# Ordering the steps of a fused attention and two-layer kernel with a small planner instead of by hand

## The chip, the cores and the metric

The kernel runs on one core of one Trainium2 chip. The time is the device time of one execution in microseconds (us); a kernel's figure is the median of its runs. Four repeats of the kernel before (312.8, 312.04, 312.56 and 313.83 us) count as slow, since they lie over 1.5% above the fastest of their rounds; medians include them, ratios do not. The engines are TensorE (PE in the profile; PEld is its weight load), VectorE (DVE), ScalarE (ACT), GpSimd (POOL) and SyncE (SP, which here issues the loads and the output writes).

## The reference

There are 8 batches of 8 heads, 576 positions and 64 columns. A small set of 32 packed queries `p` first compresses K and V into 32 rows per head; the queries then attend to those 32 rows. The result, 4608 tokens of 512 columns, goes through two layers with a squared ReLU between them.

```python
def sm_attn(qq, kk, vv):
    s = scale * np.matmul(qq, kk.transpose(0, 1, 3, 2))
    a = np.exp(s - np.max(s, axis=-1, keepdims=True))
    a = a / (np.sum(a, axis=-1, keepdims=True) + 1e-09)
    return np.matmul(a, vv)
p_packed = sm_attn(p, k, v)              # 8 x 8 x 32 x 64
x = sm_attn(q, p_packed, p_packed)       # 8 x 8 x 576 x 64, then reshaped to 4608 x 512
r = np.maximum(x @ w_in, 0.0)            # w_in  512 x 2048
out = (r * r) @ w_out                    # w_out 2048 x 512
```

Inputs and outputs are fp32; the kernel multiplies in bf16.

## The kernel before

For every batch the kernel does the same steps, and these names are used below:

- loads of k, v and q; casts to bf16; transposes of k and q on VectorE (`kT`, `qT`);
- scores of `p` against k, then P·V into the PSUM tile `ps_pp`;
- *extraction*: copies from `ps_pp` to `ppT`, the reciprocal sums `rD` and `rD8`, and eight small copies to `pq_bd` (the *pq copies*);
- *M*: the packed rows times `w_in`, so that the first layer works directly on the attention weights. Each of four M steps takes both slots of a two-slot PSUM ring that all attention steps share, and is evicted half by ScalarE and half by VectorE;
- second scores, their normalisation, and then 16 *first-layer* blocks per batch (four matmuls, a ReLU on ScalarE, a square on VectorE into `gT`);
- *second layer*: 36 output tiles of 16 matmuls each, 576 in all.

```python
def extract(self):
    ps = self.ps_pp
    for e in range(2):
        for pr in range(2):
            nc.vector.tensor_copy(self.ppT[64 * e:64 * e + 64, :, pr, :], both(ps, ...)[64 * e:64 * e + 64])
    nc.vector.reciprocal(self.rD, ps[:, 256:258])
    nc.vector.tensor_scalar_mul(self.rD8, self.rD, 0.125)
    for h in range(QH):
        pr, e = divmod(h, 2)
        for dh in range(2):
            s0 = 64 * e + 32 * dh
            dst = bd(self.pq, h, dh)
            if self.b > 1:
                nc.gpsimd.tensor_copy(dst, self.ppT[s0:s0 + 32, :, pr, :])
            else:
                nc.vector.tensor_copy(dst, both(ps, ...)[s0:s0 + 32])

def m(self, c):
    pss = [ps_att.tile([P, 512], F32, name="ps_a", tag="a") for _ in range(NQD)]   # both slots
    for h in range(QH):
        for qd in range(NQD):
            nc.tensor.matmul(pss[qd][o:o + 32, :], lhsT=self.ppT[...], rhs=w_in_b[...], start=True, stop=True)
    ...  # evict pss[0] on ScalarE and pss[1] on VectorE, scaled by rD

def fc1_unit(a, fb):
    ...  # 4 matmuls ps_h <- M, a2
    nc.scalar.activation(r[...], ps[:, :, :HALF], ACT.Relu)
    nc.vector.tensor_tensor(out=g[:, fb, o:o + S], in0=r, in1=r, op=ALU.mult)
```

The order in which steps are issued is written by hand. Lists of steps are spread over fractions of a stage and merged:

```python
def merge(lists):
    tagged = []
    for li, (x, lo, hi) in enumerate(lists):
        for i, f in enumerate(x):
            tagged.append((lo + (hi - lo) * (i + 0.5) / len(x), li, i, f))
    tagged.sort(key=lambda z: z[:3])
    for _, _, _, f in tagged:
        f()
# ... after batch 0's attention and half of its first layer:
merge([(pc[4:], 0.0, 0.02), ([s1[4], s1[7]] + s1[8:], 0.0, 0.25), (fst, 0.06, 0.55),
       ([lambda fb=fb: fc1_unit(a1, fb) for fb in range(NFB)], 0.25, 0.75), (rest, 0.55, 1),
       (pool_casts(L[2])[:2] + [lambda: prep_p(2, B)] + pool_casts(L[2])[2:], 0.55, 0.7),
       (a2.steps(), 0.6, 1.0), (L[3].dma_steps(), 0.6, 0.9)])
for b in range(2, B):          # ... one merge per batch, with fractions of its own
    ...
```

`fst` holds the casts of `w_out` (all on GpSimd), the loads of batch 2 and the second layer's first tiles.

The softmax here doesn't subtract the row's maximum and nothing guards it: scores larger than these inputs give would overflow.

Of the kernel before, what the change touches and what calls it, by code (L numbers as in the profile page):

```python
# [12 lines left out]
P = 128  # L13
D = 64
NP = 32
QH = 4
JT = 18
JP = 3
# [5 lines left out]
class Ctx:  # L24
    pass


def kernel_impl(tc, q, k, v, p, w_in, w_out, out):
# [14 lines left out]
    with ExitStack() as ctx:  # L43
# [125 lines left out]
        class Att:  # L169
            def __init__(self, b, t):  # L170
                self.b, self.t = b, t
                self.kT = att.tile([P, NQD, 2, S], BF16, name="kT", bufs=1)
                self.qT = att.tile([P, NQD, 2, S], BF16, name="qT", bufs=1)
                self.e1 = att.tile([JP * 32, NQD, G, P], BF16, name="e1")
                self.a2 = att.tile([P, NQD, S], BF16, name="a2")
                self.M = mpool.tile([P, NQD, DFF], BF16, name="M")
                self.rD = small.tile([P, NQD], F32, name="rD")
                self.ppT = small.tile([P, NQD, 2, 32], BF16, name="ppT")
                self.rD8 = small.tile([P, NQD], F32, name="rD8")
                self.pq = pq_bd[b % 2]  # L180

            def tr_q(self, qd):
                nc.vector.transpose(  # L183
                    self.qT[:, qd].rearrange("p dh (j a) -> p j dh a", a=32),
                    self.t.q[qd][:].rearrange("p (j dh dl) -> p j dh dl", dh=2, dl=32))

            def tr_k(self, qd):
                nc.vector.transpose(  # L188
                    self.kT[:, qd].rearrange("p dh (g a jp) -> p jp g dh a", jp=JP, a=32),
                    self.t.k[qd][:].rearrange("p (jp g dh dl) -> p jp g dh dl", jp=JP, dh=2, dl=32))  # L190

            def s1(self, qd, hf):
                ps = ps_att.tile([P, 512], F32, name="ps_a", tag="a")
                for gi in range(3):
                    g = hf * 3 + gi
                    for dh in range(2):
# [3 lines left out]
                                         start=(dh == 0), stop=(dh == 1))  # L200
                nc.scalar.activation(self.e1[:, qd, 3 * hf:3 * hf + 3, :], ps[:JP * 32, :3 * P],
# [18 lines left out]
            def extract(self):  # L220
                ps = self.ps_pp
# [7 lines left out]
                for h in range(QH):  # L229
                    pr, e = divmod(h, 2)  # L230
                    for dh in range(2):
                        s0 = 64 * e + 32 * dh
                        dst = bd(self.pq, h, dh)
                        if self.b > 1:
                            nc.gpsimd.tensor_copy(dst, self.ppT[s0:s0 + 32, :, pr, :])  # L235
                        else:
                            nc.vector.tensor_copy(  # L237
                                dst, both(ps, pr * 64 + 32 * e, P + (-32 if e else 32), 32)[s0:s0 + 32])

            def m(self, c):  # L240
                pss = [ps_att.tile([P, 512], F32, name="ps_a", tag="a") for _ in range(NQD)]
# [26 lines left out]
            def norm(self, qd, hf):  # L268
# [4 lines left out]
                nc.scalar.activation(ls, ps[:, :HALF], ACT.Ln)  # L273
                rs = small.tile([P, HALF], F32, name="rs", bufs=2)
                nc.scalar.activation(rs, ls, ACT.Exp, scale=-1.0)  # L275
                nc.vector.tensor_tensor(out=self.a2[:, qd, hf * HALF:(hf + 1) * HALF], in0=e2, in1=rs, op=ALU.mult)

            def kparts(self):
                return ([lambda: (expand_p(self.b, nc.vector if self.b == 0 else nc.gpsimd), self.tr_k(0)),
                         lambda: self.tr_k(1)]  # L280
                        + [lambda qd=qd, hf=hf: self.s1(qd, hf) for qd in range(NQD) for hf in range(2)])

            def steps(self):
                kp = self.kparts()
                ms = [lambda c=c: self.m(c) for c in range(NWC)]
                s2s = [lambda qd=qd, hf=hf: self.s2(qd, hf) for qd in range(NQD) for hf in range(2)]
                ns = [lambda qd=qd, hf=hf: self.norm(qd, hf) for qd in range(NQD) for hf in range(2)]
                st = [kp[0], kp[1], kp[2], kp[3], lambda: self.tr_q(0), kp[4], kp[5], lambda: self.tr_q(1)]
                st += [lambda: self.pv(0),
                       lambda: (self.pv(1), self.extract()), nop, nop, nop, ms[0], s2s[0], s2s[1], ms[1], ns[0],  # L290
                       s2s[2], ns[1], ms[2], s2s[3], ns[2], ms[3], ns[3], nop]
                return st
# [17 lines left out]
        def fc2_steps(t, alt=False):  # L310
            g = gT
# [3 lines left out]
            def mm(fb):  # L315
                if fb == 0:
                    st.ps = (ps_att.tile([P, NE], F32, name="ps_oa", tag="a") if alt
                             else ps_o.tile([P, NE], F32, name="ps_o", tag="o"))
                nc.tensor.matmul(st.ps, lhsT=g[:, fb, n0:n0 + P], rhs=w_out_b[:, fb, :],  # L319
# [9 lines left out]
            return [lambda fb=fb: mm(fb) for fb in range(NFB)]  # L329

        def merge(lists):
            tagged = []
            for li, (x, lo, hi) in enumerate(lists):
                for i, f in enumerate(x):
                    tagged.append((lo + (hi - lo) * (i + 0.5) / len(x), li, i, f))
            tagged.sort(key=lambda z: z[:3])
            for _, _, _, f in tagged:
                f()

        def nop():  # L340
            return None

        V, A, Q = nc.vector, nc.scalar, nc.gpsimd

        def pool_casts(ld):
            return ([lambda qd=qd: ld.cast_kq("k", qd, (Q,)) for qd in range(NQD)]
                    + [lambda qd=qd: ld.cast_v(qd, (Q,)) for qd in range(NQD)]
                    + [lambda qd=qd: ld.cast_kq("q", qd, (Q,)) for qd in range(NQD)])

        L = [Loads(b) for b in range(B)]  # L350
        load_p(0, 2)
        setup()
        prep_p(0, 2)
        for f in L[0].dma_steps():
            f()
        for c in range(QH):
            dma_w_in(0, c)
        a0 = Att(0, L[0])
        kp = a0.kparts()
        L[0].cast_kq("k", 0, (A, Q))  # L360
        kp[0]()
        L[0].cast_kq("k", 1, (A, Q))
        kp[2]()
        kp[1]()
        kp[3]()
        L[0].cast_v(0, (Q, V))
        kp[4]()
        L[0].cast_v(1, (Q, V))
        kp[5]()
        a0.pv(0)  # L370
        a0.pv(1)
        L[0].cast_kq("q", 0, (A, Q))
        a0.tr_q(0)
        a0.extract()
        L[0].cast_kq("q", 1, (A, Q))
        a0.tr_q(1)
        cast_w_in(0, 0, Q)
        cast_w_in(0, 1, V)
        cast_w_in(0, 2, Q)
        a0.s2(0, 0)  # L380
        a0.s2(0, 1)
        a0.s2(1, 0)
        cast_w_in(0, 3, V)
        a0.norm(0, 0)
        a0.norm(0, 1)
        a0.s2(1, 1)
        a0.norm(1, 0)
        a0.norm(1, 1)
        for c in range(QH):
            dma_w_in(1, c)  # L390
        for f in L[1].dma_steps():
            f()
        a0.m(0)
        a0.m(1)
        c1 = [lambda c=c: cast_w_in(1, c, Q) for c in range(3)]
        merge([([lambda fb=fb: fc1_unit(a0, fb) for fb in range(8)], 0, 1), (c1, 0, 1)])
        cast_w_in(1, 3, V)
        a0.m(2)
        a0.m(3)
        for c in range(4):  # L400
            dma_w_out(c)
        a1 = Att(1, L[1])
        s1 = a1.steps()
        pc = pool_casts(L[1])
        merge([([lambda fb=fb: fc1_unit(a0, fb) for fb in range(8, 16)], 0, 1),
               (pc[:2], -0.1, 0.4), (s1[:4] + s1[5:7], 0.2, 1), (pc[2:4], 0.5, 0.8)])
        fs = [fc2_steps(t, alt=False) for t in range(4)]
        fst = []
        for c in range(NFB // 2):
            def chunk(c=c):  # L410
                cast_w_out(c, Q)
                if c + 4 < NFB // 2:
                    dma_w_out(c + 4)
                if c == 3:
                    for f in L[2].dma_steps():
                        f()
                    load_p(2, B)
            fst.append(chunk)
            for t in range(2):
                for fb in (2 * c, 2 * c + 1):  # L420
                    fst.append(fs[t][fb])
        a2 = Att(2, L[2])
        rest = [nop, nop] + fs[2] + [nop, nop] + fs[3]
        merge([(pc[4:], 0.0, 0.02), ([s1[4], s1[7]] + s1[8:], 0.0, 0.25), (fst, 0.06, 0.55),
               ([lambda fb=fb: fc1_unit(a1, fb) for fb in range(NFB)], 0.25, 0.75), (rest, 0.55, 1),
               (pool_casts(L[2])[:2] + [lambda: prep_p(2, B)] + pool_casts(L[2])[2:], 0.55, 0.7), (a2.steps(), 0.6, 1.0), (L[3].dma_steps(), 0.6, 0.9)])
        cur, done = a2, 4
        for b in range(2, B):
            lists = [([lambda fb=fb: fc1_unit(cur, fb) for fb in range(NFB)], 0, 1)]
            avail = (b * S) // P  # L430
            if b + 1 < B:
                nxt = Att(b + 1, L[b + 1])
                if b == 2:
# [62 lines left out]
```

## Time and profile before

| | before |
|---|---|
| time, median | 310.55 us (3 runs, 309.9 to 312.8) |
| profiled span | 306.3 us |
| second-layer matmuls started by 110 us | 80 of 576 |

The first view is the profile page. Part 1 gives busy time, share of the span and instruction count; in part 2 each digit is one fortieth of the span (7.66 us here) in tenths of busy time, or of full clock.

```profile
PE 255.9 (84%) x1920; PEld 141.5 (46%) x1920; DVE 184.0 (60%) x306; ACT 179.7 (59%) x329; POOL 104.0 (34%) x178
...
PE   0647466689687989989999999999999999999993
...
PEclk9999969579999999999999999999999999999998
DMA  7979998950378259974188216751111121121232
```

TensorE stands at 8 or 9 tenths from the fourteenth slice on. Before that it does not, and the DMA row stays at 7 to 9 for eight slices, drops to 0 at about 69 to 77 us and comes back. The next view splits this kernel into three windows: window, length, then busy time of each engine, mean granted clock, DMA share and GB/s.

```profile
core 0: us, PE busy (x) PEld busy (x) DVE busy (x) ACT busy (x) POOL busy (x), PEclk, DMA share, GB/s
0.00:60.00 60.00, 31.14 (x245) 17.41 (x246) 41.54 (x78) 26.70 (x48) 33.68 (x47) 0.90 0.93 299
60.00:110.00 50.00, 40.04 (x296) 20.96 (x296) 29.09 (x46) 30.37 (x57) 19.00 (x35) 0.95 0.49 138
110.00:280.00 170.00, 163.17 (x1279) 93.02 (x1277) 111.41 (x179) 116.70 (x216) 51.35 (x96) 1.00 0.42 120
```

Here is TensorE's timeline of the kernel before around 100 us (start, duration, engine, line, operation, count, and in brackets the idle time before it and what ended it):

```profile
98.03 0.71 PE L246 MATMUL ps_a<-w_in_b,ppT 64*32 64x512 bf16 x8 [0.35 <-ACT e_1137 L264]
98.67 0.39 PE L319 MATMUL ps_o<-w_out_b,gT 128*128 128x512 bf16 x1
99.53 0.40 PE L260 MATMUL ps_a<-qT,pq_bd_101 128*128 128x288 bf16 x2 [0.47 <-ACT M L252]
```

From the start of M (L246) to the next start is 0.64 us. Then one second-layer matmul runs, and TensorE stands idle for 0.47 us.

A last reading, of waits on GpSimd in the kernel before (engine and line, what it waited for, us in total, times, longest), with GpSimd's timeline in the same kernel below it:

```profile
POOL pT_bd_99 L78 <- DVE pT L102: 14.2, 1, 14.2
```

```profile
81.51 1.78 POOL L78 COPY pT_bd_99<-pT 32x64 bf16<-32x64 bf16 x8 [14.19 <-DVE pT L102]
83.35 3.01 POOL L78 CAST v_b<-v_f 96x1536 bf16<-96x1536 f32 x2
```

GpSimd stands from about 67 to 81.5 us for a transpose of `p` that VectorE does late, and batch 2's v casts and batch 3's loads (first issued at 82.9 us) come after it.

### The profile page before, as it was taken

The numbers are of one execution on the slowest core, as the hardware profiler recorded it, in microseconds if no ns is written. First come the engines' busy times: TensorE is split into PE (matmuls) and PEld (weight loads), VectorE is DVE, ScalarE is ACT, GpSimd is POOL, SyncE is SP. The second block draws the span as 40 slices with busy tenths as digits, with TensorE's granted clock in tenths as the row PEclk, the third lists the DMA queues.
The fourth block names the chain that finished last, engine by engine and source line by source line (L and its number), as shares of the span: only waits on it lengthen the run. The fifth ranks groups of instructions, "written<-read, shape, count | busy, mean of one in ns | idle before, by whom it ended". The sixth has DMA issues, their size and how long they took to land.

```text
span 306.3 us, 5208 instructions
## 1 busy us (share of the span) xinstructions
PE 255.9 (84%) x1920; PEld 141.5 (46%) x1920; DVE 184.0 (60%) x306; ACT 179.7 (59%) x329; POOL 104.0 (34%) x178
## 2 busy tenths in 40 slices
PE   0647466689687989989999999999999999999993
PEld 0513234135352455445655555456545654555441
DVE  3785869534784485749685959587867634432100
ACT  3435455276566655786578647865786578655220
POOL 4443885410369404910492039202940200000000
PEclk9999969579999999999999999999999999999998
DMA  7979998950378259974188216751111121121232
GB/s 251 344 264 342 311 320 298 252 176 0 79 228 245 60 146 277 334 194 144 46 248 264 64 39 189 197 198 35 37 34 36 45 60 35 34 61 44 61 78 69
DMA packets 23353, 47.00 MB, mean 153 GB/s; under 512 B 5408, under 2 KB 11552, under 8 KB 23328
## 3 DMA queue, kind: packets, MB, share of 16 engines
q1 hardware_dynamic: 22800, 46.54, 51.4%
q8 instruction: 15, 0.25, 0.4%
q10 hardware_dynamic: 528, 0.13, 0.2%
q14 instruction: 10, 0.08, 0.1%
HBM read 37.22 MB, written 9.44 MB: 152 GB/s over the span
## 4 chain that ended last, share of the span: by engine, by line
PE 49%; DVE 18%; ACT 13%; DMA 8%; issue 4%; SPq 3%; POOL 3%; ACTq 0%; POOLq 0%; DVEq 0%
PE ps_o L319 24%; PE ps_h L302 14%; DVE kT L188 6%; DVE gT L308 5%; ACT r L306 4%; DMA kq_f<-in_q_dram 3%; PE ps_a L246 3%; PE ps_a L198 3%; ACT M L252 3%; SPq L328 3%; PE ps_a L260 2%; ACT o_sb L323 2%; DMA out_dram<-o_sb 2%; DVE qT L183 2%; DMA kq_f<-in_k_dram 2%
## 5 line engine op out<-in xcount | busy, mean ns | idle before, releaser
L319 PE MATMUL ps_o<-w_out_b,gT 128*128 128x512 bf16 x576 | 159.2, 382 | 0.0
L308 DVE TENSOR_TENSOR gT<-r 128x576 bf16<-128x576 bf16 x128 | 74.5, 586 | 65.9 <-ACT r L306 64.8
L306 ACT ACTIVATE r<-ps_h 128x576 bf16<-128x576 f32 x128 | 82.9, 651 | 44.4 <-PE ps_h L302 41.6
L319 PEld LDWEIGHTS <-gT 128*128 128x128 bf16 x576 | 54.3, 98 | 46.0 <-issue 11.5
L302 PEld LDWEIGHTS <-M 128*128 128x128 bf16 x512 | 50.8, 100 | 32.6 <-issue 2.4
L252 ACT ACTIVATE M<-ps_a,rD 128x512 bf16<-128x512 f32 x32 | 22.0, 687 | 20.9 <-PE ps_a L246 20.3
L188 DVE STREAM_TRANSPOSE kT<-k_b 128x1152 bf16<-128x1152 bf16 x16 | 32.9, 2077 | 0.0
L323 ACT COPY o_sb<-ps_o 128x512 f32<-128x512 f32 x36 | 20.8, 581 | 18.4 <-PE ps_o L319 9.7
L246 PE MATMUL ps_a<-w_in_b,ppT 64*32 64x512 bf16 x256 | 20.9, 428 | 12.5 <-DVE ppT L224 3.7
L254 DVE TENSOR_SCALAR M<-ps_a,rD 128x512 bf16<-128x512 f32 x32 | 23.8, 744 | 9.1 <-PE ps_a L246 9.1
L198 PEld LDWEIGHTS <-kT 128*96 128x96 bf16 x192 | 15.1, 132 | 24.8 <-DVE kT L188 21.8
L78 POOL CAST v_b<-v_f 96x1536 bf16<-96x1536 f32 (+1 forms) x16 | 23.4, 1478 | 5.0 <-DMA v_f<-in_v_dram 4.9
L235 POOL COPY pq_bd_102<-ppT 32x64 bf16<-32x64 bf16 x24 | 6.0, 250 | 51.8 <-DVE ppT L224 50.8
L183 DVE STREAM_TRANSPOSE qT<-q_b 128x1152 bf16<-128x1152 bf16 x16 | 21.9, 1371 | 2.5 <-POOL q_b L78 2.5
L78 POOL CAST k_b<-kq_f 128x1152 bf16<-128x1152 f32 (+1 forms) x16 | 18.3, 1162 | 6.7 <-DMA kq_f<-in_k_dram 6.4
L198 PE MATMUL ps_a<-pT_bd_99,kT 128*96 128x128 bf16 x96 | 9.1, 244 | 13.6 <-DVE kT L188 13.6
L235 POOL COPY pq_bd_101<-ppT 32x64 bf16<-32x64 bf16 x24 | 5.9, 245 | 41.4 <-DVE ppT L224 40.4
L78 POOL CAST q_b<-kq_f 128x1152 bf16<-128x1152 f32 (+1 forms) x16 | 19.1, 1210 | 1.2 <-DMA kq_f<-in_q_dram 1.2
L246 PEld LDWEIGHTS <-ppT 64*32 64x32 bf16 x256 | 5.4, 90 | 30.1 <-issue 20.4
L273 ACT ACTIVATE ls<-ps_a 128x288 f32<-128x288 f32 x32 | 13.1, 409 | 3.7 <-PE ps_a L271 3.1
L275 ACT ACTIVATE rs<-ls 128x288 f32<-128x288 f32 x32 | 14.2, 443 | 1.0
L260 PE MATMUL ps_a<-qT,pq_bd_101 128*128 128x288 bf16 x32 | 7.5, 322 | 7.1 <-DVE pq_bd_101 L237 4.1
(178 smaller groups left out, 253.6 us busy)
## 6 DMA issues: line engine op xcount, KB each, us to landing
kq_f<-in_k_dram SPq DMA_DIRECT2D x16, 576.0 KB, 5.3
v_f<-in_v_dram SPq DMA_DIRECT2D x16, 576.0 KB, 6.9
kq_f<-in_q_dram SPq DMA_DIRECT2D x16, 576.0 KB, 8.1
out_dram<-o_sb SPq DMA_DIRECT2D x144, 64.0 KB, 1.7
w_f<-in_moe_w_in_dram SPq DMA_DIRECT2D x8, 512.0 KB, 9.5
w_f<-in_moe_w_out_dram SPq DMA_DIRECT2D x8, 512.0 KB, 7.2
p_f<-in_p_dram SPq DMA_DIRECT2D x1, 384.0 KB, 14.4
p_f<-in_p_dram ACTq DMA_DIRECT2D x1, 128.0 KB, 4.1
```

Source lines behind the costliest of these rows:

```text
L78: eng.tensor_copy(dst, src)
L183: nc.vector.transpose(self.qT[:, qd].rearrange("p dh (j a) -> p j dh a", a=32), self.t.q[qd][:].rearrange("p (j dh dl) -> p j dh dl", dh=2 ...
L188: nc.vector.transpose(self.kT[:, qd].rearrange("p dh (g a jp) -> p jp g dh a", jp=JP, a=32), self.t.k[qd][:].rearrange("p (jp g dh dl) -> ...
L198: nc.tensor.matmul(ps[:JP * 32, gi * P:(gi + 1) * P], lhsT=lhsT, rhs=pT_bd[self.b % 2][:, (qd * 2 + dh) * P:(qd * 2 + dh + 1) * P], start= ...
L246: nc.tensor.matmul(pss[qd][o:o + 32, :], lhsT=self.ppT[64 * e:64 * e + 64, qd, pr, :], rhs=w_in_b[64 * e:64 * e + 64, qd * 2 + pr, c * WCH ...
L252: nc.scalar.activation(dst, pss[e], ACT.Copy, scale=self.rD[:, e:e + 1])
L254: nc.vector.tensor_scalar_mul(dst, pss[e], self.rD[:, e:e + 1])
L302: nc.tensor.matmul(ps[:, c, :HALF], lhsT=a.M[:, qd, fb * FB:(fb + 1) * FB], rhs=a.a2[:, qd, c * HALF:(c + 1) * HALF], start=(qd == 0), sto ...
L306: nc.scalar.activation(r[:].rearrange("p (c n) -> p c n", c=2), ps[:, :, :HALF], ACT.Relu)
L308: nc.vector.tensor_tensor(out=g[:, fb, o:o + S], in0=r, in1=r, op=ALU.mult)
L319: nc.tensor.matmul(st.ps, lhsT=g[:, fb, n0:n0 + P], rhs=w_out_b[:, fb, :], start=(fb == 0), stop=(fb == NFB - 1))
L323: nc.scalar.copy(o_sb, st.ps)
```

## The change

The hand order goes. Each step becomes a `Step` with durations per engine, dependencies by name, and buffer slots that it takes and gives. While the program is built, `Plan` keeps a clock for each engine queue and each slot, looks at the head of every stream, and issues the step that can start earliest on its *first* engine, or the one of best priority within 0.03 us of that. Nothing of it runs on the chip.

```diff
+class Plan:
+    def start(self, st):
+        e = st.segs[0][0]
+        t = self.free.get(e, 0.0)
+        for d in st.deps:
+            if d not in self.done:
+                return INF
+            t = max(t, self.done[d] + HOP)
+        for p, n in st.take:
...
+    def commit(self, st, t):
...
+        for seg in st.segs:
+            side = seg if isinstance(seg, list) else [seg]
+            for e, us in side:
+                b = max(t, self.free.get(e, 0.0))
+                self.free[e] = b + us          # later segments book later engines at once
...
+        st.fn()
+    def run(self):
...
+            at = [(self.start(x[1][0]), x[0], i) for i, x in enumerate(live)]
+            t0 = min(a[0] for a in at)
+            t, _, i = min((a for a in at if a[0] <= t0 + self.near), key=lambda a: (a[1], a[0]))
+            self.commit(live[i][1].pop(0), t)
...
-                        if self.b > 1:
-                            nc.gpsimd.tensor_copy(dst, self.ppT[s0:s0 + 32, :, pr, :])
-                        else:
-                            nc.vector.tensor_copy(
-                                dst, both(ps, pr * 64 + 32 * e, P + (-32 if e else 32), 32)[s0:s0 + 32])
+                        nc.vector.tensor_copy(
+                            dst, both(ps, pr * 64 + 32 * e, P + (-32 if e else 32), 32)[s0:s0 + 32])
...
+            return [Step(f"F1.{b}.{fb}", [("PE", 0.49), ("ACT", 0.66), ("DVE", 0.48)], lambda fb=fb: fc1_unit(T[b], fb),
+                         [f"M.{b}.{fb // 4}"] + [f"N.{b}.{qd}.{hf}" for qd in range(NQD) for hf in range(2)]
+                         + ([f"F2.{t}.{fb}" for t in ...] if b > 1 else []),
+                         [("h", 1), ("r", 1)], [("h", 1, 1), ("r", 2, 1)]) for fb in range(NFB)]
...
+        ld = load_steps(0) + w_in_load(0) + w_in_load(1) + load_steps(1) + w_out_load()
...
+        plan.stream(2, w_in_cast(0, (Q, V, Q, V)) + w_in_cast(1, (Q, V, Q, V)) + w_out_cast((Q, V)))
+        plan.stream(3, [x_step(b) for b in range(B)])
+        plan.stream(3, sum([tr_steps(b, "k") + tr_steps(b, "q") for b in range(B)], []))
+        plan.stream(4, sum([s1_steps(b) + pv_steps(b) for b in range(B)], []))
+        plan.stream(5, sum([m_steps(b) for b in range(B)], []))
+        plan.stream(5, sum([s2_steps(b) for b in range(B)], []))
+        plan.stream(6, sum([f1_steps(b) for b in range(B)], []))
+        plan.stream(7, sum([fc2_steps(t) for t in range(NT)], []))
+        est = plan.run()
```

Three placements change with it. Of the 16 weight casts VectorE (V) now does 8 instead of 3, and GpSimd (Q) 8 instead of 13. The pq copies of batches 2 to 7 go from GpSimd to VectorE, where they read PSUM. And GpSimd's halves of batch 0's k, q and v casts go to VectorE (k, q) and ScalarE (v).

## The prediction

> **What bounds the kernel now.** TensorE's own work, plus an early stretch in which it starves. Unit costs from the timeline: second layer 32 matmuls in 6.92 us = 0.216 us each; first layer 0.49 us per block of four; M projection 0.64 us per eight; scores 0.37 us per six; P·V 1.0 us per batch; second scores 0.24 us; norm 0.12 us. (The Trainium skill, "TensorE: Matmul & The Clock Gate", "Wait — 56ns, not 53.3ns?": N/2.4 + 2.5 ns, 215.8 ns at N = 512; the trace agrees.) Sum, an estimate: 576×0.216 + 128×0.49 + 32×(0.64+0.37+0.24+0.12) + 8×1.0 ≈ 239 us.
>
> By 110 us (windows view) only 87 of 576 second-layer matmuls, 145 of 512 first-layer ones and three batches of attention are done, about 55 us of work: some 54 us are lost. After it, 184 us of work takes 192 us; a batch period (K transpose to K transpose) is 30-32 us against 29.9 us of work: at most 8 us to gain.
>
> The early loss has a hard part: loads run at 299 GB/s over 0-60 us, DMA engines 93% busy, and the last w_out cast ends at 54.4 us; the order of loads stays, so second-layer work can't start in earnest before 48-54 us. And a soft part: batch 1's attention runs at 45-68 us, its first layer mostly at 68-90 us at a granted clock of 0.72-0.79 over 40-70 us. POOL then idles 67-81 us because pT's transpose stands late in VectorE's order; behind it batch 2's casts, batch 3's loads (83 us) and batch 2's first layer (103.7 us) are late.
>
> **What the change does.** Same arithmetic and buffers; the order is a greedy list schedule, each step as early as inputs and slots allow, second-layer matmuls as filler. Half of the weight casts from POOL to VectorE (about 1.1 us each); batches 2-7's eight pq copies from POOL (0.25 us each) to VectorE (0.22 us). VectorE then carries about 24 us per batch (estimate: kT 4.1, qT 2.7, gT 9.4, M 3.0, ppT and pq 2.8, norm 2.4), ScalarE 23 us, both under 29.9 us: off the critical path.
>
> **On the critical path.** With w_out in at 52 us, TensorE can by then have done batch 0 (14 us), batch 1's attention, part of its first layer and one second-layer tile: about 28 us. The other 211 us, and the 8 us loss end near 271 us; tail 5 us; the plain time lies 4 us above the profiled span (310.55 against 306.3), 1 us of slip: 281 us. So 30 of the 54 us come back.
>
> **Prediction: 281 us, 269 to 298.** Faster by over 2%: 0.91; within 2%: 0.06; slower: 0.03.
>
> **Right if:** second-layer matmuls done by 110 us rise from 87 to about 170; granted clock near 1.0 by 55-60 us; batch 2's first layer starts at 65-80 us; batch 3's loads issue before 75 us; POOL's 14 us wait on the pT transpose is gone; batch period still 30-32 us; DMA share over 0-50 us still 0.9. **Wrong if** the gain sits in the batch period.
>
> **What would make it wrong.** The plan's durations are short of the trace's: M 0.40 against 0.64 us, K transpose 1.4 against 2.05, gT 0.48 against 0.59, loads faster than 299 GB/s, output writes free. VectorE is strict FIFO (same page, first table), so a w_out cast placed too early there blocks squares and transposes behind it; output writes queue behind loads.

## More of the kernel before

The busy figures of TensorE must not be read as work. The ends of matmuls are modelled, so overlapping ones count waiting and filling as busy.

## The result, and the profile after

| | before | after |
|---|---|---|
| time, median (same rounds) | 310.23 us (4 runs) | 291.3 us (4 runs) |
| ratio, 95% interval | | 0.9413 (0.9314 to 0.9511) |
| profiled span | 306.3 us | 289.3 us |
| second-layer matmuls by 110 us | 80 | 129 |
| GpSimd's wait for the transpose of `p` | 14.2 us | 1.6 us |

A ratio is the mean time of one kernel's fast runs over the mean of the other's of the same rounds, so it isn't quite the ratio of the medians. Here it leaves out the 312.8 us of the kernel before.

The same rows of the page, of the changed kernel (a slice is 7.23 us):

```profile
PE 251.1 (87%) x1920; PEld 139.7 (48%) x1920; DVE 192.2 (66%) x363; ACT 177.2 (61%) x331; POOL 78.6 (27%) x119
...
PE   0526884789999999999998999999998999999993
...
PEclk9999997879999999999999999999999999999999
DMA  7977999999969693155049960271120201120222
```

The DMA row no longer has a hole before 110 us, and TensorE's row reaches 9 in the tenth slice. The early slices are hardly better. The windows of the changed kernel say the same:

```profile
0.00:60.00 60.00, 32.58 (x253) 18.40 (x254) 46.42 (x86) 27.21 (x48) 22.41 (x35) 0.94 0.92 292
60.00:110.00 50.00, 48.76 (x418) 26.40 (x415) 39.21 (x74) 34.64 (x69) 28.31 (x48) 0.97 0.91 267
110.00:280.00 170.00, 165.18 (x1239) 93.07 (x1240) 106.57 (x205) 114.22 (x213) 27.85 (x36) 1.00 0.32 91
```

And TensorE's timeline of the changed kernel, in a stretch of M steps:

```profile
64.14 0.41 PE L314 MATMUL ps_a<-w_in_b,ppT 64*32 64x512 bf16 x8
64.48 2.12 PE L370 MATMUL ps_o<-w_out_b,gT 128*128 128x512 bf16 x9
66.53 0.41 PE L314 MATMUL ps_a<-w_in_b,ppT 64*32 64x512 bf16 x8
66.87 1.90 PE L370 MATMUL ps_o<-w_out_b,gT 128*128 128x512 bf16 x8
```

Here an M step takes 0.34 us from its start to the next start, not 0.64 (of all 32 M steps 22 do so, in the kernel before 12), and eight or nine second-layer matmuls fill the 2 us until the next M can have its two slots. No idle time is shown.

**Where the time came from.** To compare runs, I count the work that TensorE has done by a given time, as an estimate worked out from the traces: each matmul that has started counts the time from its start to the next start where nothing waits. That is 0.2155 us for a second-layer matmul, 0.49 for a first-layer block, 0.342 for an M step, 0.335 for six score matmuls, 0.243 and 0.122 for a second score and a norm, and 1.0 for a batch's P·V. The sum is 576×0.2155 + 128×0.49 + 32×(0.342 + 0.335 + 0.243 + 0.122) + 8×1.0 = 228.2 us. What a stretch has beyond the work done in it is lost time:

| us lost by TensorE, profiled run | 0 to 60 us | 60 to 110 us | 110 us to the last matmul |
|---|---|---|---|
| before | 42.9 | 16.7 | 13.8 |
| after | 40.6 | 5.1 | 10.6 |

The change takes 17.1 us out: 2.3 before 60 us, 11.6 between 60 and 110, and 3.2 after. A part of this loss is the clock. A stretch's length times the missing share of its mean granted clock (0.90 and 0.95 before, 0.94 and 0.97 after) is 6.2 and 2.3 us before, 3.4 and 1.7 us after, and nothing from 110 to 280 us in either; as an estimate, that is the most that the clock took. So the 2.3 us gained before 60 us may be the clock alone.

The first 60 us are nearly as bad as they were, and the steady part still loses 10.6 us. The experiments ask about these two remainders, and about what was gained. In some traces of the experiments up to 33 of the 1920 matmul records are missing; their counts are scaled up by kind, so differences under about 1 us in this measure mean nothing.

### The profile page after: what moved, and what is told of

Same layout as the page of the kernel before. It is cut to its first block, busy times and chain, and to the rows that moved or that the text cites. A ratio compares the mean times of both kernels' runs of the same rounds, so it can differ in the third digit from the quotient of the medians.

```text
span 289.3 us, 5225 instructions
## 1 busy us (share of the span) xinstructions
PE 251.1 (87%) x1920; PEld 139.7 (48%) x1920; DVE 192.2 (66%) x363; ACT 177.2 (61%) x331; POOL 78.6 (27%) x119
## 4 chain that ended last, share of the span: by engine, by line
PE 61%; DVE 24%; ACT 7%; DMA 3%; issue 2%; SPq 1%; DVEq 0%
PE ps_o L370 30%; PE ps_h L355 19%; DVE kT L254 7%; PE ps_a L314 4%; DVE gT L361 3%; ACT r L359 3%; PE ps_a L264 2%; DVE pq_bd_101 L304 2%; PE ps_a L328 2%; DVE qT L248 2%; DVE pq_bd_102 L304 2%; DVE ppT L294 2%; DMA out_dram<-o_sb 2%; DMA p_f<-in_p_dram 1%; PE ps_pp L279 1%
## 5 line engine op out<-in xcount | busy, mean ns | idle before, releaser
L370 PE MATMUL ps_o<-w_out_b,gT 128*128 128x512 bf16 x576 | 153.0, 385 | 5.8 <-DVE w_out_b L145 2.4
L361 DVE TENSOR_TENSOR gT<-r 128x576 bf16<-128x576 bf16 x128 | 67.0, 536 | 34.3 <-ACT r L359 32.3
L359 ACT ACTIVATE r<-ps_h 128x576 bf16<-128x576 f32 x128 | 79.8, 653 | 14.7 <-PE ps_h L355 9.7
L355 PEld LDWEIGHTS <-M 128*128 128x128 bf16 x512 | 48.7, 98 | 27.0 <-issue 7.0
L374 ACT COPY o_sb<-ps_o 128x512 f32<-128x512 f32 x36 | 20.9, 582 | 30.7 <-PE ps_o L370 19.3
L145 POOL CAST k_b<-kq_f 128x1152 bf16<-128x1152 f32 x14 | 16.1, 1152 | 56.4 <-DVE kT L254 45.1
L145 POOL CAST q_b<-kq_f 128x1152 bf16<-128x1152 f32 x14 | 15.9, 1144 | 43.9 <-issue 42.1
L145 POOL CAST v_b<-v_f 96x1536 bf16<-96x1536 f32 x14 | 20.4, 1469 | 7.3 <-DMA v_f<-in_v_dram 6.3
L314 PE MATMUL ps_a<-w_in_b,ppT 64*32 64x512 bf16 x256 | 17.3, 412 | 5.3 <-DVE pq_bd_102 L304 1.8
L248 DVE STREAM_TRANSPOSE qT<-q_b 128x1152 bf16<-128x1152 bf16 x16 | 21.2, 1349 | 0.0
L344 ACT ACTIVATE rs<-ls 128x288 f32<-128x288 f32 x32 | 14.2, 443 | 1.0
L294 DVE CAST ppT<-ps_pp 64x64 bf16<-64x64 f32 x32 | 5.7, 217 | 11.6 <-PE ps_pp L284 11.5
L355 PE MATMUL ps_h<-a_285,M 128*128 128x288 bf16 x64 | 10.6, 305 | 0.9 <-ACT r L359 0.6
## 6 DMA issues: line engine op xcount, KB each, us to landing
p_f<-in_p_dram SPq DMA_DIRECT2D x1, 384.0 KB, 13.8
```

The lines of the kernel that those rows point to most:

```text
L145: eng.tensor_copy(dst, src)
L248: nc.vector.transpose(self.qT[:, qd].rearrange("p dh (j a) -> p j dh a", a=32), self.t.q[qd][:].rearrange("p (j dh dl) -> p j dh dl", dh=2 ...
L314: nc.tensor.matmul(pss[qd][o:o + 32, :], lhsT=self.ppT[64 * e:64 * e + 64, qd, pr, :], rhs=w_in_b[64 * e:64 * e + 64, qd * 2 + pr, c * WCH ...
L355: nc.tensor.matmul(ps[:, c, :HALF], lhsT=a.M[:, qd, fb * FB:(fb + 1) * FB], rhs=a.a2[:, qd, c * HALF:(c + 1) * HALF], start=(qd == 0), sto ...
L359: nc.scalar.activation(r[:].rearrange("p (c n) -> p c n", c=2), ps[:, :, :HALF], ACT.Relu)
L370: nc.tensor.matmul(st.ps, lhsT=gT[:, fb, n0:n0 + P], rhs=w_out_b[:, fb, :], start=(fb == 0), stop=(fb == NFB - 1))
```

## The experiments

All kernels but the last computed the right result. The starting point for most is the changed kernel, which was run once more, unedited, beside the second group. e1, e2, e5 and e8 shared one chip; a_control, e3, e4 and e10 another; e13, e15 and e16 a third; e17 a fourth. Across chips the ratios are compared, not the times.

| run | edit | median us | ratio to before, 95% | lost 0–60 | 60–110 | after 110 |
|---|---|---|---|---|---|---|
| a_control | none | 292.46 | 0.9455 (0.9383 to 0.9528) | 40.7 | 7.0 | 10.5 |
| e3_pq_pool | pq copies back on GpSimd | 284.28 | 0.9184 (0.9106 to 0.9262) | 41.6 | 5.4 | 4.0 |
| e16_pq_sbuf | pq copies on VectorE, from SBUF | 293.64 | 0.9481 (0.9439 to 0.9523) | 41.1 | 5.6 | 12.6 |
| e15_before_pq_dve | before, pq copies on VectorE | 313.79 | 1.0142 (1.0099 to 1.0185) | 43.4 | 22.6 | 14.6 |
| e5_before_p_early | before, `p` prepared early | 309.33 | 1.0013 (0.9929 to 1.0098) | 42.8 | 19.5 | 15.0 |
| e1_kt_early | batch 1's k transposes earlier | 294.69 | 0.9564 (0.9486 to 0.9642) | 41.2 | 13.9 | 7.2 |
| e2_wo_pool | `w_out` casts on GpSimd only | 293.25 | 0.9514 (0.9460 to 0.9568) | 41.9 | 4.8 | 11.8 |
| e8_kt_wo | both of these | 288.99 | 0.9351 (0.9282 to 0.9421) | 38.3 | 4.6 | 8.7 |
| e4_vq_act | batch 1's v, q casts on ScalarE | 291.07 | 0.9415 (0.9339 to 0.9491) | 40.1 | 5.6 | 10.0 |
| e10_ld_wo | e2 and batch 1's k, v loaded earlier | 293.27 | 0.9506 (0.9409 to 0.9602) | 40.1 | 5.0 | 13.3 |
| e13_kt_wo_pq | e8 and e3 | 282.00 | 0.9115 (0.9069 to 0.9160) | 38.8 | 4.1 | 4.3 |
| e17_no_wout | e1 and e3, no `w_out` (wrong) | 284.99 | 0.9230 (0.9200 to 0.9259) | 37.8 | 5.9 | 7.6 |

The record's verdict at 2% is "faster" for e1, e2, e8, e13, e16 and e17, "same" for e5 and e15, and "unclear" for the four runs on the chip of a_control, where two of the seven repeats of the kernel before were slow. Those four are therefore compared with each other.

### Question 1: what does the move of the pq copies to VectorE cost?

The prediction held that VectorE, with 24 us of work in a batch of about 30, had room for them. The opposite reading, which is not the rival written down for e3: they stand in the middle of a chain from P·V to the next transposes and evictions, in an engine that works in order, and cost time there.

**e3_pq_pool**, the copies back on GpSimd; the plan's durations and so its order are untouched.

```diff
-                        nc.vector.tensor_copy(
-                            dst, both(ps, pr * 64 + 32 * e, P + (-32 if e else 32), 32)[s0:s0 + 32])
+                        if self.b > 1:
+                            nc.gpsimd.tensor_copy(dst, self.ppT[s0:s0 + 32, :, pr, :])
+                        else:
+                            nc.vector.tensor_copy(
+                                dst, both(ps, pr * 64 + 32 * e, P + (-32 if e else 32), 32)[s0:s0 + 32])
```

> Undo one part: the eight pq copies of batches 2-7 go back to POOL, nothing else moves. As predicted (off the critical path): within 1.5 us of the control. Rival: these copies sit between P.V and the second scores of every batch, POOL does them behind its casts, and the time rises by 2-5 us.

Measured: 284.28 us against the control's 292.46 on the same chip, 8.2 us less; the two intervals of the ratios lie apart. Both branches of the expectation missed: one had the time within 1.5 us, the other 2 to 5 us longer. Of the 7.2 us between the two profiled runs 6.5 are after 110 us, where the lost time falls from 10.5 to 4.0 us. One extraction shows how. First VectorE in the changed kernel (start, duration, engine, line, operation, count), then TensorE in it:

```profile
148.69 0.73 DVE L294 CAST ppT<-ps_pp 64x64 bf16<-64x64 f32 x4
...
150.28 1.85 DVE L304 CAST pq_bd_101<-ps_pp 32x64 bf16<-32x64 f32 x8
152.16 2.10 DVE L254 STREAM_TRANSPOSE kT<-k_b 128x1152 bf16<-128x1152 bf16 x1
154.29 0.75 DVE L322 TENSOR_SCALAR M<-ps_a,rD 128x512 bf16<-128x512 f32 x1
```

```profile
151.20 0.39 PE L314 MATMUL ps_a<-w_in_b,ppT 64*32 64x512 bf16 x1
152.18 0.41 PE L314 MATMUL ps_a<-w_in_b,ppT 64*32 64x512 bf16 x7 [0.60 <-DVE pq_bd_101 L304]
```

The same place with the copies on GpSimd (e3_pq_pool), VectorE and then TensorE:

```profile
149.31 0.73 DVE L294 CAST ppT<-ps_pp 64x64 bf16<-64x64 f32 x4
...
150.35 2.10 DVE L254 STREAM_TRANSPOSE kT<-k_b 128x1152 bf16<-128x1152 bf16 x1
152.32 0.75 DVE L325 TENSOR_SCALAR M<-ps_a,rD 128x512 bf16<-128x512 f32 x1
```

```profile
151.81 0.41 PE L317 MATMUL ps_a<-w_in_b,ppT 64*32 64x512 bf16 x8
```

In the changed kernel VectorE is in the extraction from 148.69 to 152.16, 3.5 us, where the plan counts 2.0. M needs both PSUM slots and `ps_pp` still holds one, so all but its first matmul wait until the last pq copy has read it. The transpose of k, which is next in VectorE's order, and M's eviction behind that start late too. From the first `ppT` copy to M's eviction is 5.60 us (154.29 − 148.69); with the copies on GpSimd it is 3.01 us (152.32 − 149.31). This isn't the same in every batch: over batches 2 to 7 the difference is 2.6, −0.4, 2.6, 0.7, 2.6 and 0.7 us, 8.8 us in all. That is near the 8.2 us gained, but that each of these us delays TensorE isn't shown.

**e16_pq_sbuf** parts two explanations: the held PSUM slot, or VectorE's time. The copies stay on VectorE but read `ppT` in SBUF, so that the slot is free once `ppT` and `rD` are read.

```diff
-                        nc.vector.tensor_copy(
-                            dst, both(ps, pr * 64 + 32 * e, P + (-32 if e else 32), 32)[s0:s0 + 32])
+                        nc.vector.tensor_copy(dst, self.ppT[s0:s0 + 32, :, pr, :])
```

> Edit to the changed kernel: the eight pq copies stay on VectorE, but read the SBUF copy ppT instead of PSUM. Putting them back on POOL gained 8 us (ratio 0.918 against 0.9455 of the control). Slot theory: the loss comes from holding the P.V accumulator, one of two attention PSUM slots, for 1.85 us longer, so that the M projection's second half waits (about 0.99 us in the trace); reading ppT frees it, and most of the 8 us come back: ratio 0.918-0.93, 285-288 us. Load theory: it's the 1.85 us of VectorE time itself ahead of the transposes and M's evictions: ratio 0.938-0.947, 291-293 us. In between if the SBUF copies are shorter than 0.22 us each.

Measured: 293.64 us, ratio 0.9481, no gain over the control (0.9455); the load theory is the nearer one, though its range ended at 0.947. VectorE and TensorE in e16_pq_sbuf:

```profile
150.82 3.23 DVE L304 COPY pq_bd<-ppT 32x64 bf16<-32x64 bf16 x8
154.09 2.07 DVE L254 STREAM_TRANSPOSE kT<-k_b 128x1152 bf16<-128x1152 bf16 x1
```

```profile
151.74 0.41 PE L313 MATMUL ps_a<-w_in_b,ppT 64*32 64x512 bf16 x8
156.22 1.40 PE L264 MATMUL ps_a<-pT_bd,kT 128*96 128x128 bf16 x12 [2.23 <-DVE kT L254]
```

M no longer waits: its eight matmuls run as one group. But the transpose still comes late, and now the scores wait 2.23 us for it. So the slot by itself isn't what the 8 us hang on; VectorE's order is the explanation left. The experiment isn't clean, since in this place the eight copies took 3.23 us instead of 1.85, beside casts on GpSimd. Its profiled run also had a granted clock of 0.98 from 110 to 280 us, which by the estimate above is up to 3.4 of the 12.6 us lost there. What it shows is that freeing the slot doesn't bring the time back while VectorE is occupied as long or longer.

**e15_before_pq_dve** does this part of the change alone, on the kernel before: the branch for GpSimd is removed, as in the diff of the change.

> One part of the change alone, on the kernel before: its eight pq copies of batches 2-7 go from POOL to VectorE, order as it was. If the copies are costly in themselves: slower by 3-8 us, 313-318 us. If they are costly only in the planned order, where the M projection is placed to start as soon as the plan thinks P.V done: within 2 us of 310 us, since the hand order has three empty steps between P.V and M.

Measured: 313.79 us against 309.91, 1.4% slower; the six runs lie above all eleven of the kernel before. The profiled run can't place the cost. It loses its extra time between 60 and 110 us (22.6 against 16.7), but its granted clock was 0.83 there against 0.95, which by the estimate above is up to 8.6 us against 2.3. The clock isn't the whole difference: at 0.954 over the whole run e15 took 314.0 us, the kernel before 311.07. From the first `ppT` copy to M's eviction e15 takes longer in batch 2 alone (4.26 us against 1.48), and up to 0.3 us less or the same in the five batches after it. In the hand order, then, the copies lengthen this chain once and not in the steady part.

### Question 2: did GpSimd's 14 us wait cause the late batches?

The prediction reads the wait as the cause of the late casts, loads and first layer of batch 2. The rival: everything there is late for other reasons, and GpSimd merely stands in line.

**e5_before_p_early**, on the kernel before: `p` of batches 2 to 7 is loaded and prepared early.

```diff
             dma_w_in(1, c)
+        load_p(2, B)
         for f in L[1].dma_steps():
...
         cast_w_in(1, 3, V)
+        prep_p(2, B)
         a0.m(2)
...
-                    load_p(2, B)
...
-               (pool_casts(L[2])[:2] + [lambda: prep_p(2, B)] + pool_casts(L[2])[2:], 0.55, 0.7), ...
+               (pool_casts(L[2]), 0.55, 0.7), ...
```

> Edit to the kernel before: p of batches 2-7 is loaded ahead of batch 1's data and its cast and transpose stand in the queues before batch 0's third M projection, nothing else. If the 60-110 us stretch of the kernel before was lost to the late pT transpose (POOL idle 67-81 us behind it), batch 2's attention moves up by 5-10 us and the time falls to 301-306 us. Rival (the hand order loses there for other reasons: batch 3's loads behind output writes, M projections of batch 1 and 2 running one by one): less than 3 us gained, 308-311 us.

Measured: 309.33 us, the same as before (308.03 on that chip). The profiled run was the slowest of the four (312.3 us), with a granted clock of 0.87 from 60 to 110 us against 0.95; but at like clocks over the whole run (0.964 and 0.965) e5 took 307.71 us and the kernel before 307.82. GpSimd's timeline of e5_before_p_early answers to the two lines shown for the kernel before:

```profile
63.34 2.32 POOL L78 COPY pT_bd<-pT 32x64 bf16<-32x64 bf16 x8
65.72 1.46 POOL L78 CAST v_b<-v_f 96x1536 bf16<-96x1536 f32 x1
```

The wait is gone and the v casts stand at 65.7 us instead of 83.35. Still the k transpose of batch 2 came at 84.5 us (before: 81.3) and the loads of batch 3 at 86.5 (before: 82.9). The wait was the longest single one on GpSimd, and its removal gained nothing. That the hand order itself places those steps (`a2.steps()` and `L[3].dma_steps()` stand at 0.6 of the merge and later) is read from the code, not tested.

### Question 3: what holds the first 60 us?

Both kernels lose over 40 us there. In the changed kernel, batch 1's k is cast by 36.1 us, but its transposes run at 47.6 and 50.1 us, behind squares of batch 0. VectorE of the changed kernel, and before it GpSimd of the same kernel:

```profile
32.22 1.15 POOL L145 CAST k_b<-kq_f 128x1152 bf16<-128x1152 f32 x1 [1.77 <-DMA kq_f<-in_k_dram]
34.98 1.15 POOL L145 CAST k_b<-kq_f 128x1152 bf16<-128x1152 f32 x1 [1.62 <-DMA kq_f<-in_k_dram]
```

```profile
37.02 10.02 DVE L361 TENSOR_TENSOR gT<-r 128x576 bf16<-128x576 bf16 x12
46.97 0.68 DVE L145 CAST w_out_b<-w_f 128x1024 bf16<-128x1024 f32 x1
47.57 2.08 DVE L254 STREAM_TRANSPOSE kT<-k_b 128x1152 bf16<-128x1152 bf16 x1
```

Theory S, starvation in the plan: a first-layer step begins on TensorE and is ranked by its start there, although its square books VectorE at once, so such steps are taken before a transpose that begins on the busy VectorE. The plan's own figures show this for batch 1: it has k ready at 28.0 us and its transpose at 40.3. (The plan's own end is 266.6 us, 22.7 under the profiled span.) Theory P: twelve squares take 10.02 us, 0.84 each, because GpSimd's casts block them, and that is the delay. Theory F, from the prediction: a floor, since the second layer can't start in earnest before `w_out` is loaded and cast.

**e1_kt_early** tests S: the last eight first-layer blocks of batch 0 wait for batch 1's k transposes.

```diff
-                         [f"M.{b}.{fb // 4}"] + ...
+                         ([f"Tk.1.{fb // 4 - 2}"] if b == 0 and fb >= 8 else []) + [f"M.{b}.{fb // 4}"] + ...
```

> Edit: in the changed kernel's plan, blocks 8-11 of batch 0's first layer must come after batch 1's first K transpose, blocks 12-15 after its second. Theory S (starvation: a step that begins on TensorE always looks earlier than one that begins on VectorE, so batch 1's transposes stand behind all sixteen squares of batch 0): the first K transpose of batch 1 starts at 34-38 us instead of 47.6, batch 1's first layer at 62-68 us instead of 74.7, and the time falls by 4 to 8 us, to 283-287 us. Rival D (data: w_out and batch 1's loads come late, so the order in the first 60 us doesn't matter): the transposes move, the time stays within 2 us of 291. The plan itself now puts the last w_out cast later, which works against the gain.

Measured: 294.69 us, not better than the changed kernel. The transposes did come earlier (42.4 and 44.3 us), and batch 1's first layer at 66.3 us instead of 74.7. But the last `w_out` cast on VectorE ended at 68.9 us (59.4 in the changed kernel), only 9 second-layer matmuls were done by 60 us instead of 17, and the stretch from 60 to 110 us lost 13.9 us instead of 5 to 7.

**e2_wo_pool** takes the `w_out` casts off VectorE.

```diff
-... + w_out_cast((Q, V)))
+... + w_out_cast((Q,)))
```

> Edit: all eight w_out casts on POOL instead of POOL and VectorE in turn. Theory S: the last w_out cast ends at 55-57 us instead of 59.4, batch 1's K transposes start perhaps 1 us earlier, and the time changes by less than 3 us, since the transposes still stand behind the squares. Rival D: w_out is what TensorE waits for in the first 60 us, so its earlier casts show in full, 2-4 us. Rival P (POOL's casts hold back VectorE's squares): more POOL casts, slower by 1-3 us.

Measured: 293.25 us, no gain. The last `w_out` cast ended at 54.9 us, batch 1's k transpose still only at 49.6 us.

**e8_kt_wo** is both edits together.

> Both edits together (K transposes of batch 1 early, w_out casts on POOL). Theory S: the gain of the first edit without its drawback: batch 1's first layer starts at 60-66 us, 22 us of work done by 60 us rise to 27-30, time 280-285 us. Rival D: within 3 us of 291 us, or the gain of the w_out edit alone.

Measured: 288.99 us, ratio 0.9351 against 0.9413 and 0.9455 of the two runs of the changed kernel. The intervals overlap, so this is a hint, and the time also lies within rival D's 3 us. VectorE in e8_kt_wo shows the transposes in place:

```profile
36.83 4.08 DVE L361 TENSOR_TENSOR gT<-r 128x576 bf16<-128x576 bf16 x4
40.84 3.99 DVE L254 STREAM_TRANSPOSE kT<-k_b 128x1152 bf16<-128x1152 bf16 x2
```

Though they are 6.7 us earlier, TensorE's work by 60 us is up by only 2.3 us (21.7 against 19.4). Theory S is true of the plan, and a small part of the loss.

**e4_vq_act** tests P: the v and q casts of batch 1 go from GpSimd to ScalarE, after batch 0's first layer.

```diff
+        who = lambda b: (A, V) if b == 0 else (A,) if b == 1 else (Q,)
+        cs = {b: cast_steps(b, "k", ...) + cast_steps(b, "v", who(b)) + cast_steps(b, "q", who(b)) for b in range(B)}
+        for st in cs[1][2:]:
+            st.deps.append(f"F1.0.{NFB - 1}")
```

> Edit to the changed kernel: batch 1's v and q casts run on ScalarE after batch 0's last first-layer block instead of on POOL; VectorE's order in the first 60 us stays the same but for one swap. Theory P (in the first 60 us VectorE is late because POOL's casts hold back its squares: in the changed kernel the 22 squares that overlap a POOL instruction take 0.91 us, the others 0.457): the sixteen squares of batch 0 end at 40-42 us instead of 47, batch 1's first K transpose starts at 41-43 us instead of 47.6, and the time falls by 2-5 us. Theory S alone (the order of the queue is what matters): the transpose starts no earlier than 45 us, time within 1.5 us of the control.

Measured: 291.07 us against the control's 292.46, no difference. Here is VectorE in e4_vq_act:

```profile
41.67 1.00 DVE L361 TENSOR_TENSOR gT<-r 128x576 bf16<-128x576 bf16 x2 [0.39 <-ACT r L359]
...
46.20 2.09 DVE L254 STREAM_TRANSPOSE kT<-k_b 128x1152 bf16<-128x1152 bf16 x1
```

The squares that no GpSimd instruction overlaps take about 0.46 us each, and now they wait for ScalarE's ReLUs, which take 0.65 to 0.70 us a block. The transpose came at 46.2 us instead of 47.5 in the control. The blocking is real but not the limit, because ScalarE is right behind it.

That it is real shows in the changed kernel's trace: of its 128 squares the 22 that overlap a GpSimd instruction by more than 50 ns take 0.913 us on average, the other 106 take 0.457. In the kernel before it is 0.867 (41 squares) and 0.454 (87). The Trainium skill, "SBUF — State Buffer", section "SBUF: two separate sides", says that the port pair shared by VectorE and GpSimd is "an exclusive lock, not a bandwidth split", and counts a VectorE operation with two SBUF inputs among those that take it against a GpSimd operation that reads SBUF. A square has two SBUF inputs and a cast reads SBUF, so the trace agrees.

**e10_ld_wo** brings batch 1's k and v in before the second half of `w_in`.

```diff
-        ld = load_steps(0) + w_in_load(0) + w_in_load(1) + load_steps(1) + w_out_load()
+        l1 = load_steps(1)
+        ld = load_steps(0) + w_in_load(0) + l1[:4] + w_in_load(1) + l1[4:] + w_out_load()
```

(with e2's edit)

> Edit to the changed kernel: batch 1's k and v are loaded before the second half of w_in, and w_out casts all run on POOL. This gives batch 1's K transposes a free VectorE by arrival time, not by a rule in the plan. Theory S/chain (what was missing in the first 60 us is batch 1's attention, a chain of over 20 us from the K transpose to the first layer): K transposes of batch 1 at 24-30 us, first layer of batch 1 at 58-64 us instead of 74.7, work done by 60 us 26-30 us instead of 21, time 282-287 us. Rival D (w_out's arrival sets when TensorE is fed): work by 60 us stays below 23 us and the time within 3 us of the control.

Measured: 293.27 us, no gain, though the transposes of k stood at 31.3 and 34.1 us. Batch 1's first layer started only at 69.7 us, and by 50 us only 32 of batch 0's 64 first-layer matmuls were done, where the changed kernel had all 64: what one batch gained in the order, the other paid.

**e13_kt_wo_pq** joins e8 and e3 into the best version that these findings suggest.

> The two edits that helped, together: pq copies of batches 2-7 on POOL, and batch 1's K transposes early with w_out casts on POOL. If they act in different stretches (the one after 110 us, the other before 60 us) they add: 0.918 x 0.935/0.9435 = 0.91, 281-283 us. If they overlap: 284 us, as with the first alone.

Measured: 282.00 us (280.41 to 283.82), ratio 0.9115. It beats both kernels, and its ratio lies 0.0236 below that of e8 (about 7 us), so the pq copies cost about the same on top of the other edits as alone (0.0271 from the control to e3). Its lost time is 38.8, 4.1 and 4.3 us.

**e17_no_wout** tests theory F in the plainest way. It starts from e1 and e3, loads and casts no `w_out` at all, and lets the second layer multiply by `w_in`'s first 512 columns, which are there early. The result is wrong (relative error 2.65).

```diff
-                nc.tensor.matmul(st.ps, lhsT=gT[:, fb, n0:n0 + P], rhs=w_out_b[:, fb, :],
+                nc.tensor.matmul(st.ps, lhsT=gT[:, fb, n0:n0 + P], rhs=w_in_b[:, fb % QH, :NE],
...
-                    [f"F1.{b}.{fb}" for b in bs] + [f"WO.{fb // 2}"],
+                    [f"F1.{b}.{fb}" for b in bs] + [f"WI.0.{fb % QH}"],
...
-        ld = load_steps(0) + w_in_load(0) + w_in_load(1) + load_steps(1) + w_out_load()
+        ld = load_steps(0) + w_in_load(0) + w_in_load(1) + load_steps(1)
```

> A take-away, wrong result on purpose: as the run that joins the two helpful edits (282.0 us, ratio 0.9115), but the second layer multiplies by slices of w_in, so w_out is neither loaded nor cast, and second-layer work is open from about 33 us on. If w_out's arrival (44-56 us) is what keeps TensorE short of work in the first 60 us (the hard part of the prediction): work done by 60 us rises from 21 to 28-33 us and the time falls by 7-12 us, to 270-275 us. If batch 0's and 1's attention in the plan's order is the limit, filler or not: work by 60 us stays below 25 us and the time falls by less than 4 us.

Measured: 284.99 us, ratio 0.9230, so slower than e13 (0.9115). Without 4 MB of loads and eight casts, TensorE had done 22.2 us of work by 60 us, against 21.2 in e13; that fits the second branch (below 25 us), but the time rose instead of falling. So in this order theory F falls: the arrival of `w_out` isn't what holds the first 60 us. The run isn't clean, though. It keeps e1's rule, so batch 0's first layer stands still from 39.6 to 46.1 us behind batch 1's transposes, and its plan itself ends later (268.5 us against 264.5 for e13). On the changed kernel's own order the take-away wasn't run; there TensorE's waits for `w_out` casts come to 4.8 us.

What does hold them is seen only in part. TensorE's longest waits in the first 60 us of the changed kernel (us in total, times, longest):

```profile
PE ps_a L264 <- DVE kT L254: 10.7, 3, 9.6
PE ps_a L328 <- DVE qT L248: 5.9, 2, 5.2
```

These are batch 0's k and q transposes. Of TensorE's 27.4 us of idle time before 60 us, 17.0 lie in the first 24 us (before: 15.3 of 28.8), and no experiment touched that start. The third change of placement falls in it: VectorE does its halves of batch 0's q casts at 18.8 us, after the extraction, where GpSimd did its halves from 13.2 us on, and batch 0's first layer starts at 30.6 us instead of 27.6. Whether that costs time wasn't tested. Beyond the start, the traces show a long chain inside each batch: from k's transpose to the batch's first layer it is 7.5 to 30.6 us in batch 0 and 47.6 to 74.7 in batch 1 of the changed kernel, 40.8 to 69.9 in e8. Three single causes were taken away without much gain, and a second step of the chain was behind each. No run took the whole chain apart.

## Why the prediction was right or wrong

The direction and the size class were right: 281 us was predicted with a range of 269 to 298, and 291.3 was measured. The 10 us between them have causes that can be named. Part of the closeness is luck, because errors offset each other: the work was put 10.8 us too high, the loss by 52 us too low (24 us, where the changed kernel lost 36.6), and the "4 us" from span to plain time compares two different runs (the profiled run took 308.44 us, 2.1 above its span).

**Right.** GpSimd's wait for `p` fell from 14.2 to 1.6 us, batch 3's loads are issued from 65.9 us instead of 82.9, the DMA share over the first 60 us stayed at 0.92, and the batch period stayed within its band on average (first layer to first layer: 30.0 us, 31.9 before). Taken from K transpose to K transpose, as the prediction did, it averages 30.7 us from batch 2 on (30.0 before), but single ones run from 22.6 to 40.4. Most of the gain lies before 110 us: 13.9 of 17.1 us. The skill's figure for a matmul of N = 512 (215.8 ns by the formula in the section that the prediction names) was right to use: 0.2155 us in these traces.

**Wrong, the step "both under 29.9 us: off the critical path".** This was said of VectorE and ScalarE with the pq copies added. The average load was judged well enough, and the conclusion didn't follow from it. Undoing the move gives 8.2 us on the changed kernel and about 7 us on e8; it costs 1.4% on the kernel before. The copies lie between P·V and the transposes and evictions on an engine that works in order, and there 1.85 us of extra work came out as 2.6 us more from the extraction to M's eviction in three of six batches (5.60 against 3.01 us in the one shown), 0.7 in two and none in one.

**Wrong, the step "second-layer work can't start in earnest before 48-54 us".** It was called the hard part of the early loss. With `w_out` taken away altogether (e17) nothing is gained. The number built on it, 28 us of work by 52 us, was far too high: the changed kernel had done 15.4 us by 52 and 19.4 by 60 us (before: 15.8 and 17.1). What stood in its place is TensorE's idle start (17.0 us by 24 us) and a late batch 1, whose k transposes run at 47.6 and 50.1 us. Moving these 6.7 us earlier (e8) brought 2.3 us of work by 60 us, so most of this loss stays unexplained. With it fell its signs: second-layer matmuls by 110 us went from 80 to 129 and not to 170 (the 87 in the prediction counts those that cross a window's edge twice), the clock was 0.83 over 40 to 70 us and not near 1.0 by 55 to 60, and batch 2's first layer started at 106.3 us (before: 103.7), not at 65 to 80. So "30 of the 54 us come back" was the mis-sized term: 13.9 came back before 110 us.

**Wrong, the reading that "behind it batch 2's casts, batch 3's loads (83 us) and batch 2's first layer (103.7 us) are late".** The early `p` of e5 removed the wait and moved none of the times that mattered.

**Wrong, the term "M projection 0.64 us per eight".** In the kernel before, half of the 32 M steps take 0.64 us or more from their start to the next start, but 12 show 0.34: in most of the others all but the first matmul wait for a PSUM slot, and the wait lies within a merged row of eight. 32×0.3 = 9.6 us of waiting were counted as work; with 1.1 us in the scores (0.37 against 0.335) this makes most of the step from 228.2 to 239 us. Therefore "at most 8 us to gain" after 110 us was too low: 13.8 us were lost there, and e3 gets it down to 4.0. This error and the pq copies partly hid each other, since the change got back 3.2 us of a stretch in which the order alone, as e3 has it, gets back 9.8.

**Not isolated.** That fillers between dependent steps brought the 11.6 us between 60 and 110 us is read from the timelines (8 or 9 second-layer matmuls between two M steps where the hand order had one) and not shown by a run of its own. Rivals that no run parts from it are the earlier loads (267 GB/s in that stretch, 138 before) and the weight casts moved off GpSimd.

## What to carry to other kernels

Take the cost of a step from the occurrence that waits least, start to next start, and not from a merged row of the profile. Room on an engine's average doesn't put work off the critical path: look at which in-order chain the moved work stands in, and test it by undoing just that move. A list scheduler that ranks by the start on a step's first engine can starve steps that begin on a busy later one, so compare in its own plan when a step was ready and when it was started, but measure what the cure is worth, because here a second limit stood close behind each one.

## What the Trainium skill lacked or had wrong

- "TensorE: Matmul & The Clock Gate", section "Back-to-back issue gap", gives a sustained spacing of about 131 ns per matmul at N = 512 and says that the formula of about 216 ns over-counts there. In these traces the second layer, which loads weights for each matmul, runs at 0.2155 us at full clock (the median from start to start is 0.216 us in both kernels). The formula was right, the 131 ns weren't seen.
- The same page, section "What's actually happening", has the granted clock either at half or at full speed. The clock records of all traces here hold 0.5 and 1.0 only, so a window's mean (0.83 over 40 to 70 us in the changed kernel) stands for about a third of the window at half speed, an estimate: (1 − 0.83) / 0.5. The page doesn't say how to read such a mean.
- "SBUF — State Buffer", section "SBUF: two separate sides", states the lock between VectorE and GpSimd, and the page has no time for this pair. Here a square of 128x576 took 0.913 us on average beside a GpSimd instruction and 0.457 without, at most 2.77 us in the changed kernel.
- No page that I looked up warns that a merged group of matmuls can hide a wait for a PSUM slot within it: eight M matmuls took 0.64 us with it and 0.34 without.
- No page that I looked up gives the cost of a transpose on VectorE by its output layout: 128x1152 took 2.08 to 2.09 us on average into the layout of `kT` and 1.35 to 1.37 us into that of `qT`.
